# A fifth block of the first channel product computed from seven small products, and a second batch's x kept in DRAM

## The chip, the cores and the metric

The kernel runs on one core of one Trainium2 chip. The metric is device time in microseconds. One execution in the profile is a trace of every instruction on the core's engines: TensorE (PE for its matmuls, PEld for the loads of its stationary operand), VectorE (DVE), ScalarE (ACT), GpSimd (POOL) and SyncE (SP), which issues most transfers.

## The reference, cut to what matters

Inputs are q, k, v of shape (4, 8, 768, 64): batch, heads, sequence, head size. Each query and key is assigned to one of 16 clusters, attention is kept between equal clusters only, and the heads are put side by side to x of shape (4, 768, 512). A mixer block follows:

```
xt = x.transpose(0, 2, 1)
h = np.maximum(xt @ w_tok1, 0.0) @ w_tok2
u = x + h.transpose(0, 2, 1)
h2 = np.maximum(u @ w_ch1, 0.0) @ w_ch2
return (u + h2).astype(np.float32)
```

w_ch1 is 512 x 1536, w_ch2 is 1536 x 512, all in float32. The change lies in the product u @ w_ch1, here called the first channel product.

## The kernel before, in words

The program has three stages. Attention takes sixteen pairs of heads, up to about 316 us in the trace. The token stage (to about 394 us) computes the products with w_tok1 and w_tok2. The channel stage takes the rest.

The channel stage runs over the four batches in the order 0, 2, 3, 1, and in each over three parts. A part takes, by ch1_pair, one third of the columns of w_ch1, and then, by ch2_chunks, the second channel product for these columns, added to x. Products are made in blocks by a scheme with seven products in place of eight (Winograd's form of Strassen's): the table SEVEN names, for each of the seven, the PSUM tag, the left block or block sum (A11, S1 ...), the right one (B11, T1 ...) and where it goes. Left blocks come from the weights, and their sums are made once. Right blocks come from uT, the transposed u, and their sums are made for each batch by u_sums.

The first part of batch 0 runs ch1_plain: seven products, each for i = 0 and 1 (two halves of 128 of its columns), each with two matmuls of 128 x 384 that accumulate. The other eleven parts run ch1_sets, which goes one level deeper. It writes big(X, name, ...) for a product made plainly (A11 B11, S2 T2, S3 T3), and for the four others it takes "sets" of seven small products on blocks half as large (128 x 192 output): Y (A12 B21), P (S1 T1), Z (S4 B22) and X (A22 T4). set_lefts and set_rights build the block names, and left and right sums of a set (l2 in the tile w1ss, r2 in the tile uTss) are made by set_left_sums and set_right_sums on VectorE.

How a set is put together matters for the steps below. small(...) is one matmul. direct(bank, set) is two of them (c11 and c12) side by side in one bank. chain(q, set, name, x) makes one small product into the bank q, where the products of one set add up (p1, then u2, c22, c21), and then adds the bank, as it is at that moment, to x in SBUF with one VectorE sum. So the next product of the same chain can only start when that sum has read the bank. column(z, set, x) makes the product p5 and adds it to two places with one sum. relu and the copies run on ScalarE.

The order of work on each engine is the order in which the code records it; each engine takes its instructions in that order, and semaphores connect them. Between products, between() takes a recorded step from the list late (the rest of the part before) and some from others (sums for coming work), and big() also takes a step of beside, which turns the next batch's u.

Space in SBUF is given by pools that stand in a stack. The x of batches 1 and 3 share: xs lists four tiles, one of them (batch 1) in x1pool, which closes with the token stage; batch 1's x is written to the DRAM tile spill at the end of the first pair of batches, and read back into batch 0's tile after batch 0 is done. x of batch 3 stays in xpool. The pools w2sums (sums of w_ch2, w1ss, uTss) and mlp (the hidden blocks) take the space of the closed pools.

Lines to know in the profile: L798 is a big product, L871 a small one, L966 a product of ch2_chunks, L566 add and L563 sub on VectorE, L810 relu.

Of the kernel before, what the change touches and what calls it, by code (L numbers as in the profile page):

```python
# [8 lines left out]
F32 = mybir.dt.float32  # L9
# [10 lines left out]
P = 128  # L20
# [30 lines left out]
def kernel(  # L51
# [47 lines left out]
    x1pool = pool("x1pool", 1, tokens)  # L99
    spilled = pool("spilled", 1, space=bass.MemoryType.DRAM)  # L100
    tokpool = pool("tokpool", 1, tokens)
    staging = fast.enter_context(ExitStack())
    stage = pool("stage", 2, staging)
    attention = fast.enter_context(ExitStack())
# [25 lines left out]
    }  # L130

    state = {}
    spill = spilled.tile([P, NJ, DM], F32, name="spill")
    xs = [(x1pool if b == 1 else xpool).tile([P, NJ, DM], F32, name=f"x{b}") for b in range(B)]


    def load(g):
# [461 lines left out]

    def set_lefts():
        if "l2" not in pools:
            pools["l2"] = pools["w2sums"].tile([P, 4, 3, HS], F32, name="w1ss")
        l2 = pools["l2"]
        yx = W["ch1"].rearrange("p f (i r c) -> p f i r c", i=2, r=2)[:, 2:4]
        pz = pools["w1s"][:, 0:3:2].rearrange("p i f (r c) -> p f i r c", r=2)
        for n, both in enumerate((yx, pz)):
            blocks = [both[:, f, :, r] for r in range(2) for f in range(2)]
            sums_ = [l2[:, 2 * n : 2 * n + 2, m] for m in range(3)]  # L610
            yield dict(
                zip(("A11", "A12", "A21", "A22", "S1", "S2", "S4", "S3"), blocks + sums_ + blocks[2:3])
            )
# [6 lines left out]
    def set_rights():  # L620
        uT, R, r2 = pools["uT"], pools["R"], pools["r2"]
        yz = uT[:, :, 2:4].rearrange("p n f (k t) -> p n f k t", k=2)
        x, p = (R[name].rearrange("p f (k t) -> p f k t", k=2) for name in ("T4", "T1"))
        for blocks, sums_ in (
            ([yz[:, :, f, k] for f in range(2) for k in range(2)], [r2[:, 0:2, m] for m in range(3)]),
            ([x[:, f, k] for f in range(2) for k in range(2)], [r2[:, 2, m] for m in range(3)]),
            ([p[:, f, k] for f in range(2) for k in range(2)], [r2[:, 3, m] for m in range(3)]),
        ):
            yield dict(
                zip(("B11", "B12", "B21", "B22", "T1", "T2", "T4", "T3"), blocks + sums_ + blocks[1:2])  # L630
            )

    def set_right_sums():

        pools["r2"] = pools["w2sums"].tile([P, 4, 3, HS // 2], F32, name="uTss")
        return [list(winograd_right(blocks)) for blocks in set_rights()]

    def set_blocks():

        (yx, pz), (yz, x, p) = (list(y) for y in (set_lefts(), set_rights()))  # L640
        left = {name: {k: a[:, i] for k, a in two.items()} for two, i, name in
                ((yx, 0, "Y"), (yx, 1, "X"), (pz, 0, "P"), (pz, 1, "Z"))}
        right = {"Y": {k: b[:, 0] for k, b in yz.items()}, "Z": {k: b[:, 1] for k, b in yz.items()},
                 "X": x, "P": p}
        return left, right

    def token_weights():
# [98 lines left out]
    def by_turns(n, product, of, last=False, after=()):  # L746


        if last:
            order = "p1 0 p1 1 p1 2 p5 0 p5 1 p5 2 c11 0 c11 1 u2 0 u2 1 u2 2 c12 0 c12 1 c11 2 c12 2 "  # L750
            order += "c22 0 c22 1 c21 0 c22 2 c21 1 c21 2"
        else:
            order = "p1 0 p1 1 p1 2 p5 0 p5 1 p5 2 c11 0 c11 1 u2 0 u2 1 u2 2 c12 0 c12 1 "
            order += "c22 0 c22 1 c22 2 c12 2 c11 2 c21 0 c21 1 c21 2"
        order = order.split()
        banks, after = {}, dict(after)
        for m in range(len(order) // 2):
            name, i = order[2 * m], int(order[2 * m + 1])
            tag, a, r, to = SEVEN[name]
            if name in FIRST:  # L760
                banks[tag, i] = ptile(tag, n)
            product(banks[tag, i], a, r, i, name in FIRST)
            x = of(to, i)
            add(x, banks[tag, i], x)
            if m in after:
                after[m]()
            between()

    def tok2_chunks(b, after=()):

# [13 lines left out]
    def ch1_pair(part, sets, beside):  # L784


        h2 = pools["h2"] = {
            k: pools["mlp"].tile([P, 2, HS], F32, name="h" + k)
            for k in ("A11", "A12", "A22", "S1", "S2", "S3", "S4")
        }  # L790
        p5, c12 = (pools["mlp"].tile([P, 2, HS], F32, name=k) for k in ("p5", "c12"))
        A, R = pools["A"], pools["R"]
        a11, a12, a22 = h2["A11"], h2["A12"], h2["A22"]

        def product(psum, a, r, i, start):
            c = slice((part + 3 * i) * P, (part + 3 * i + 1) * P)
            for k in range(2):
                nc.tensor.matmul(  # L798
                    psum, lhsT=A[a][:, k, c], rhs=R[r][:, k],
                    start=start and k == 0, stop=k == 1, skip_group_check=not start,  # L800
                )

        def big(psum, a, r, i, start):
            product(psum, a, r, i, start)
            between()
            if a != "A11" and beside:
                beside.pop(0)()

        def relu(x):
            nc.scalar.activation(out=x, in_=x, func=ACT.Relu)  # L810


        def sum_1():
            nc.vector.scalar_tensor_tensor(
                out=h2["S1"], in0=c12, scalar=0.0, in1=a22, op0=ALU.max, op1=ALU.add
            )

        def sum_2():
            sub(h2["S2"], h2["S1"], a11)

        def sums_34():
            nc.vector.scalar_tensor_tensor(
                out=h2["S3"], in0=c12, scalar=0.0, in1=a11, op0=ALU.max, op1=ALU.subtract
            )
            sub(h2["S4"], a12, h2["S2"])

        (ch1_sets if sets else ch1_plain)(
            part, product, big, relu, a11, a12, a22, p5, c12, sum_1, sum_2, sums_34
        )

    def ch1_plain(part, product, big, relu, a11, a12, a22, p5, c12, sum_1, sum_2, sums_34):
        X, Z = {}, {}
        for i in range(2):
            X[i] = ptile("X", HS)
# [26 lines left out]
        late_(0)  # L861
        late.append(lambda: late_(1))

    def ch1_sets(part, product, big, relu, a11, a12, a22, p5, c12, sum_1, sum_2, sums_34):

        left, right = set_blocks()
        n0, n1 = slice(0, HS // 2), slice(HS // 2, HS)
# [45 lines left out]
        nc.scalar.copy(out=p5[:, 1, n1], in_=pz[:, n0])  # L913
        relu(a11[:, 0])
        add(p5[:, 0, n1], pz[:, n0], p5[:, 0, n1])
        add(c12[:, 0], X[0], p5[:, 0])
        big(X[1], "S2", "T2", 1, False)
        chain(yq, "Y", "c22", a11[:, 1, n1])
        chain(pq, "P", "c22", p5[:, 1, n1])
        direct(ybe, "Z")  # L920
        chain(yq, "Y", "c21", a11[:, 1, n0])
        small(pq[:, n0], "P", "c21", False)
        nc.scalar.copy(out=p5[:, 1, n0], in_=pq[:, n0])
        relu(a11[:, 1])
        add(c12[:, 0], ybe, c12[:, 0])
        chain(yz, "Z", "p1", c12[:, 0, n0])
        add(c12[:, 1], X[1], p5[:, 1])
        big(X[0], "S3", "T3", 0, False)
        add(a22[:, 0], X[0], p5[:, 0])
        relu(a22[:, 0])  # L930
        chain(yz, "Z", "u2", c12[:, 0, n1])
        column(pbe, "Z", c12)
        big(X[1], "S3", "T3", 1, False)
        add(a22[:, 1], X[1], p5[:, 1])
        relu(a22[:, 1])
        chain(yz, "Z", "c22", c12[:, 1, n1])
        direct(X[0], "X", False)
        nc.scalar.copy(out=a12[:, 0], in_=X[0])
        small(X[1][:, n0], "X", "c21", False)
        nc.scalar.copy(out=a12[:, 1], in_=X[1])  # L940
        chain(yz, "Z", "c21", c12[:, 1, n0])
        chain(yq, "X", "p1", a12[:, 0, n0])
        sum_1()

        def late_1():
            chain(yq, "X", "u2", a12[:, 0, n1])
            column(pz, "X", a12)
            sum_2()

        def late_2():  # L950
            chain(yq, "X", "c22", a12[:, 1].rearrange("p (k t) -> p k t", k=2))
            relu(a12)
            sums_34()

# [167 lines left out]
    for b in (0, 2):  # L1122
# [26 lines left out]
        if b == 2:  # L1149
            take(turning, len(turning))  # L1150
            usums = u_sums()
            tok2_chunks(b, {13: lambda: next(usums)})
        else:
            left_weights()
            others += left_sums(0)
            tok2_chunks(b)
            nc.sync.dma_start(spill, xs[1])
            turning = list(u_steps(0))
    assert not weights
    token_stack.close()  # L1160
# [5 lines left out]
    for n, b in enumerate(batches):  # L1166
        turning = []
        for part in range(3):
# [33 lines left out]
                (fits_count if part else fits)()  # L1202
            if part == 2 and not last:

                yz, x, p = steps
                yz[0]()
                yz[1]()
                next(usums)

                others += [lambda: next(usums)] * 2  # L1210
                others.append(lambda: [step() for step in (yz[2], p[2], yz[3], p[3])])
                others += [lambda: None, lambda: (x[0](), x[1]()), lambda: (x[2](), x[3]())]
                if n == 0:
                    xs[1] = xpool.tile([P, NJ, DM], F32, name="x0")
                    nc.sync.dma_start(xs[1], spill)


    def general():
# [213 lines left out]
```

## Time and profile before

The time is 823.15 us, the median of 3 runs (822.59 to 823.39). The profiled execution spans 821.6 us.

| engine | busy, us | share of the span | instructions |
|---|---|---|---|
| PE (matmuls) | 814.2 | 99% | 4348 |
| PEld (weight loads) | 535.5 | 65% | 4348 |
| DVE | 631.1 | 77% | 1206 |
| ACT | 374.7 | 46% | 573 |
| POOL | 30.7 | 4% | 28 |

The page's rows are groups of instructions: line, engine, operation, output and input by the program's names, count, busy time and mean duration in ns, and idle time before them with what ended it. A busy share is a mean over stages, so a stage is read from its own stretch of time. Matmuls overlap in the pipeline, so a row's mean duration (326 ns for 128 x 192, 486 for 128 x 384) is longer than the distance from one to the next. A float32 matmul of the program stands as two MATMULs in the trace. DMA moves 63.41 MB in all, most of it before the channel stage; the one spill of 1536 KB landed 5.1 us after its issue, and its load back 7.0 us after.

### The profile page before, as it was taken

Reading aid. Unit: us, or ns where it says so; the run is one execution under the profiler, and the core shown is the slowest. Engines: PE = TensorE matmul, PEld = TensorE weight load, DVE = VectorE, ACT = ScalarE, POOL = GpSimd, SP = SyncE. Lnnn points to the kernel's source line nnn. Section 1 sums busy time; section 2 is a strip of 40 time slices with the busy share of each in tenths; the row PEclk is TensorE's granted clock in tenths of the full one; section 3 lists DMA queues with packets and bytes.
Section 4 is the critical chain, followed back from the end, with each engine's and each line's share of the span. In section 5 each row is a group of like instructions: output and inputs, shape, how many; then the busy total and the mean of one; then the engine's idle time right before and its main releaser. Section 6 shows DMA issues by size and latency. Waiting matters only on the chain.

```text
span 821.6 us, 11693 instructions
## 1 busy us (share of the span) xinstructions
PE 814.2 (99%) x4348; PEld 535.5 (65%) x4348; DVE 631.1 (77%) x1206; ACT 374.7 (46%) x573; POOL 30.7 (4%) x28
## 2 busy tenths in 40 slices
PE   8999999999999999999999999999999999999997
PEld 4444444444444444444588888888888888888876
DVE  6879898989898978859797788755777566775665
ACT  5588776777878776127202154121441204511120
POOL 1001010111011000000000000000000000000000
PEclk9999999999999999999999999999999999999999
DMA  8797666768676434143000025000240001400002
GB/s 156 142 162 135 140 142 122 149 139 163 130 160 137 95 104 122 51 127 79 0 1 1 5 45 183 1 0 1 38 117 0 1 1 30 125 1 1 1 0 81
DMA packets 184258, 63.41 MB, mean 77 GB/s; under 512 B 172800, under 2 KB 176896, under 8 KB 183936
## 3 DMA queue, kind: packets, MB, share of 16 engines
q1 hardware_dynamic: 182592, 62.18, 34.7%
q8 instruction: 36, 0.59, 0.3%
q10 hardware_dynamic: 1600, 0.39, 0.2%
q14 instruction: 30, 0.25, 0.1%
HBM read 36.21 MB, written 7.86 MB: 54 GB/s over the span
## 4 chain that ended last, share of the span: by engine, by line
PE 98%; DVE 1%; issue 0%; ACT 0%; DVEq 0%; ACTq 0%
PE sc L413 19%; PE av L455 15%; PE pX L966 15%; PE pX L798 12%; PE pZ L966 7%; PE ph L534 5%; PE pY L871 5%; PE pZ L871 4%; PE pX L871 4%; PE pY L966 4%; PE pX L774 3%; PE small L491 2%; PE pZ L774 1%; PE small L304 1%; PE pZ L798 1%; PE pY L774 1%
## 5 line engine op out<-in xcount | busy, mean ns | idle before, releaser
L437 ACT ACTIVATE ex<-sc 128x768 f32<-128x768 f32 x192 | 151.0, 812 | 27.2 <-PE sc L413 15.5
L413 PE MATMUL sc<-qkT 64*128 64x384 f32 x768 | 155.3, 483 | 0.0
L445 DVE TENSOR_TENSOR sum<-sum,ex 128x768 f32<-128x768 f32 x128 | 127.8, 999 | 27.1 <-ACT ex L437 14.9
L455 PE MATMUL av<-ex,va 128*64 128x384 f32 x768 | 127.4, 488 | 0.0
L566 DVE TENSOR_TENSOR x<-pX,x 128x256 f32<-128x256 f32 (+1 forms) x168 | 75.8, 458 | 38.1 <-PE pX L966 37.6
L455 PEld LDWEIGHTS av<-ex,va 128*64 128x64 f32 x768 | 53.7, 137 | 71.7 <-issue 67.6
L413 PEld LDWEIGHTS sc<-qkT 64*128 64x128 f32 x768 | 67.8, 187 | 38.3 <-issue 38.0
L810 ACT ACTIVATE hA<-hA 128x384 f32<-128x384 f32 (+1 forms) x57 | 34.0, 597 | 85.4 <-DVE hA L566 85.1
L566 DVE TENSOR_TENSOR hA<-pY,hA 128x192 f32<-128x192 f32 (+1 forms) x90 | 36.7, 407 | 45.4 <-PE pY L871 42.7
L798 PE MATMUL pX<-uT,wc 128*128 128x384 f32 x192 | 69.8, 487 | 0.0
L894 ACT COPY hA<-pX 128x384 f32<-128x384 f32 x11 | 5.3, 479 | 131.3 <-PE pX L798 131.3
L413 PE MATMUL sc<-ohT 64*128 64x384 bf16 x384 | 62.4, 323 | 0.0
L462 ACT COPY avrows<-av 128x768 uint16<-128x768 uint16 x32 | 25.5, 797 | 44.4 <-PE av L455 44.4
L566 DVE TENSOR_TENSOR x<-pZ,x 128x256 f32<-128x256 f32 (+1 forms) x84 | 36.4, 455 | 11.4 <-PE pZ L966 11.3
L798 PEld LDWEIGHTS pX<-uT,wc 128*128 128x128 f32 x192 | 35.4, 190 | 14.7 <-issue 0.6
L534 PE MATMUL ph<-x,wt 128*128 128x512 f32 x96 | 41.6, 593 | 0.0
L413 PEld LDWEIGHTS <-ohT 64*128 64x128 bf16 x384 | 18.7, 94 | 33.8 <-issue 9.6
L966 PE MATMUL pX<-wc,hA 128*128 128x256 f32 x144 | 36.9, 380 | 0.3 <-ACT hA L940 0.3
L711 ACT COPY uT<-ucols 128x768 uint16<-128x768 uint16 x32 | 33.2, 1049 | 4.7 <-DMA ucols<-urows 4.7
L966 PE MATMUL pZ<-wc,hS 128*128 128x256 f32 x144 | 35.0, 379 | 0.0
L966 PE MATMUL pY<-wc,hA 128*128 128x256 f32 x144 | 35.0, 379 | 0.0
L798 PE MATMUL pX<-uTs,w1s 128*128 128x384 f32 x96 | 34.9, 486 | 0.0
(189 smaller groups left out, 1310.8 us busy)
## 6 DMA issues: line engine op xcount, KB each, us to landing
raw<-in_moe_w_ch_dram SPq DMA_DIRECT2D x24, 512.0 KB, 4.5
va<-in_v_dram SPq DMA_DIRECT2D x16, 384.0 KB, 3.7
out_dram<-x SPq DMA_DIRECT2D x24, 256.0 KB, 2.3
qk<-in_k_dram SPq DMA_DIRECT2D x60, 96.0 KB, 4.0
qk<-in_q_dram SPq DMA_DIRECT2D x60, 96.0 KB, 3.5
raw<-in_moe_w_tok_dram SPq DMA_DIRECT2D x3, 512.0 KB, 4.1
raw<-in_moe_w_tok_dram SPq DMA_DIRECT2D x4, 384.0 KB, 3.8
spill<-x SPq DMA_DIRECT2D x1, 1536.0 KB, 5.1
```

What stands on the lines that cost most here:

```text
L413: nc.tensor.matmul(sc[:, h, 0:HS], lhsT=src[rows, 1, j], rhs=src[rows, 0, HJ * qh : HJ * qh + HJ], start=start, stop=not start,)
L437: nc.scalar.activation(out=ex, in_=sc[:, :, 0:HS], func=ACT.Exp, scale=SM_SCALE)
L445: nc.vector.tensor_tensor(out=acc, in0=acc if j > 1 else st["ex", qh, 0], in1=st["ex", qh, j], op=ALU.add)
L455: nc.tensor.matmul(av[h * D : (h + 1) * D], lhsT=st["va"][:, h, j], rhs=ex[:, h], start=(j == 0), stop=(j == NJ - 1),)
L534: nc.tensor.matmul(pf, lhsT=W["tok1"][:, j, t * P : (t + 1) * P], rhs=xs[b][:, j], start=(j == 0), stop=(j == NJ - 1),)
L566: nc.vector.tensor_tensor(out=dst, in0=a, in1=b, op=ALU.add)
L711: nc.scalar.copy(out=out, in_=pools.pop(("ucols", i)).rearrange("p w j t -> p w (j t)"))
L774: nc.tensor.matmul(psum, lhsT=A[a][:, i], rhs=R[r], start=start, stop=True, skip_group_check=not start,)
L798: nc.tensor.matmul(psum, lhsT=A[a][:, k, c], rhs=R[r][:, k], start=start and k == 0, stop=k == 1, skip_group_check=not start,)
L810: nc.scalar.activation(out=x, in_=x, func=ACT.Relu)
L871: nc.tensor.matmul(psum, lhsT=left[which][a][:, part * P : part * P + P], rhs=right[which][r], start=start, stop=True, skip_group_check=no ...
L966: nc.tensor.matmul(psum, lhsT=h2[a][:, k, i * P : (i + 1) * P], rhs=Bw[w][:, part + 3 * k], start=start and k == 0, stop=k == 1, skip_grou ...
```

## The change

A fifth of the seven products of the first channel product, S3 T3, is no longer made by big products but as a set, U, of seven small ones. Its bank is not shared with the other big products as before: U is put together in a new SBUF tile u3, like P in p5, and added from there to a22 and a12. S3 is a block of w_ch1 itself, T3 a block of u's sums; U's own sums need a fifth place in w1ss and in uTss. The set's products are recorded among those of Y and Z, so the second half of ch1_sets has a new order. To make room in SBUF, x of batch 3 also goes into a pool that closes after the token stage; it is written to DRAM at the end of the token stage and read back after batch 0, and batch 1 is then read back after batch 2. The remaining edits spread recorded steps: by_turns now passes between() a number that empties others over its steps, and a new helper aside() takes a step of beside.

```diff
-    spill = spilled.tile([P, NJ, DM], F32, name="spill")
-    xs = [(x1pool if b == 1 else xpool).tile([P, NJ, DM], F32, name=f"x{b}") for b in range(B)]
+    spill = {b: spilled.tile([P, NJ, DM], F32, name=f"spill{b}") for b in (1, 3)}
+    homes = (xpool, x1pool, xpool, x3pool)
+    xs = [homes[b].tile([P, NJ, DM], F32, name=f"x{b}") for b in range(B)]
...
-            pools["l2"] = pools["w2sums"].tile([P, 4, 3, HS], F32, name="w1ss")
+            pools["l2"] = pools["w2sums"].tile([P, 5, 3, HS], F32, name="w1ss")
...
+            ([u[:, f, k] for f in range(2) for k in range(2)], [r2[:, 4, m] for m in range(3)]),
...
-            between()
+            between(-(-len(others) // max(len(order) // 2 - m, 1)))
...
-        add(c12[:, 0], X[0], p5[:, 0])
+
+        add(a22[:, 0], X[0], p5[:, 0])
         big(X[1], "S2", "T2", 1, False)
         chain(yq, "Y", "c22", a11[:, 1, n1])
         chain(pq, "P", "c22", p5[:, 1, n1])
-        direct(ybe, "Z")
+        direct(ybe, "U")
+        nc.scalar.copy(out=u3[:, 0], in_=ybe)
         chain(yq, "Y", "c21", a11[:, 1, n0])
         small(pq[:, n0], "P", "c21", False)
         nc.scalar.copy(out=p5[:, 1, n0], in_=pq[:, n0])
         relu(a11[:, 1])
-        add(c12[:, 0], ybe, c12[:, 0])
-        chain(yz, "Z", "p1", c12[:, 0, n0])
-        add(c12[:, 1], X[1], p5[:, 1])
-        big(X[0], "S3", "T3", 0, False)
-        add(a22[:, 0], X[0], p5[:, 0])
+        chain(pbe, "U", "p1", u3[:, 0, n0])
+        add(a22[:, 1], X[1], p5[:, 1])
+        nc.scalar.copy(out=c12[:, 1], in_=a22[:, 1])
+        between()
+        direct(pz, "Z")
+        chain(pbe, "U", "u2", u3[:, 0, n1])
+        add(c12[:, 0], pz, a22[:, 0])
+        small(yz[:, n0], "U", "p5")
+        nc.scalar.copy(out=u3[:, 1, n1], in_=yz[:, n0])
+        add(u3[:, 0, n1], yz[:, n0], u3[:, 0, n1])
+        chain(yq, "Z", "p1", c12[:, 0, n0])
+        chain(pbe, "U", "c22", u3[:, 1, n1])
+        add(a22[:, 0], a22[:, 0], u3[:, 0])
+        chain(yq, "Z", "u2", c12[:, 0, n1])
+        between()
+        small(pbe[:, n0], "U", "c21", False)
+        nc.scalar.copy(out=u3[:, 1, n0], in_=pbe[:, n0])
         relu(a22[:, 0])
-        chain(yz, "Z", "u2", c12[:, 0, n1])
-        column(pbe, "Z", c12)
-        big(X[1], "S3", "T3", 1, False)
-        add(a22[:, 1], X[1], p5[:, 1])
+        column(pq, "Z", c12)
+        chain(yq, "Z", "c22", c12[:, 1, n1])
+        add(a22[:, 1], a22[:, 1], u3[:, 1])
         relu(a22[:, 1])
-        chain(yz, "Z", "c22", c12[:, 1, n1])
         direct(X[0], "X", False)
-        nc.scalar.copy(out=a12[:, 0], in_=X[0])
+        add(a12[:, 0], X[0], u3[:, 0])
         small(X[1][:, n0], "X", "c21", False)
-        nc.scalar.copy(out=a12[:, 1], in_=X[1])
-        chain(yz, "Z", "c21", c12[:, 1, n0])
-        chain(yq, "X", "p1", a12[:, 0, n0])
+        add(a12[:, 1], X[1], u3[:, 1])
+        chain(yq, "Z", "c21", c12[:, 1, n0])
+        chain(ybe, "X", "p1", a12[:, 0, n0])
         sum_1()
+        aside()
...
+            nc.sync.dma_start(spill[3], xs[3])
         else:
...
-            nc.sync.dma_start(spill, xs[1])
+            nc.sync.dma_start(spill[1], xs[1])
...
-                others += [lambda: None, lambda: (x[0](), x[1]()), lambda: (x[2](), x[3]())]
-                if n == 0:
-                    xs[1] = xpool.tile([P, NJ, DM], F32, name="x0")
-                    nc.sync.dma_start(xs[1], spill)
+                others += [lambda: (u[0](), u[1]()), lambda: (u[2](), u[3]())]
+                others.append(lambda: [step() for step in x])
+                if n < 2:
+
+                    later = batches[n + 2]
+                    xs[later] = xpool.tile([P, NJ, DM], F32, name=f"x{b}")
+                    nc.sync.dma_start(xs[later], spill[later])
```

More of the change, by code (lines that the diff above doesn't have):

```diff
@@ L101 @@
     tokpool = pool("tokpool", 1, tokens)
+    x3pool = pool("x3pool", 1, tokens)
     staging = fast.enter_context(ExitStack())
@@ L603, in set_lefts @@
         if "l2" not in pools:
-            pools["l2"] = pools["w2sums"].tile([P, 4, 3, HS], F32, name="w1ss")
+            pools["l2"] = pools["w2sums"].tile([P, 5, 3, HS], F32, name="w1ss")
         l2 = pools["l2"]
-        yx = W["ch1"].rearrange("p f (i r c) -> p f i r c", i=2, r=2)[:, 2:4]
+        w1 = W["ch1"].rearrange("p f (i r c) -> p f i r c", i=2, r=2)
         pz = pools["w1s"][:, 0:3:2].rearrange("p i f (r c) -> p f i r c", r=2)
-        for n, both in enumerate((yx, pz)):
+        for n, both in ((slice(0, 2), w1[:, 2:4]), (slice(2, 4), pz), (slice(4, 5), w1[:, 0:2, 1:2])):
             blocks = [both[:, f, :, r] for r in range(2) for f in range(2)]
-            sums_ = [l2[:, 2 * n : 2 * n + 2, m] for m in range(3)]
+            sums_ = [l2[:, n, m] for m in range(3)]
             yield dict(
@@ L622, in set_rights @@
         yz = uT[:, :, 2:4].rearrange("p n f (k t) -> p n f k t", k=2)
-        x, p = (R[name].rearrange("p f (k t) -> p f k t", k=2) for name in ("T4", "T1"))
+        x, p, u = (R[name].rearrange("p f (k t) -> p f k t", k=2) for name in ("T4", "T1", "T3"))
         for blocks, sums_ in (
@@ L633, in set_right_sums @@
     def set_right_sums():
-        pools["r2"] = pools["w2sums"].tile([P, 4, 3, HS // 2], F32, name="uTss")
+        pools["r2"] = pools["w2sums"].tile([P, 5, 3, HS // 2], F32, name="uTss")
         return [list(winograd_right(blocks)) for blocks in set_rights()]
     def set_blocks():
-        (yx, pz), (yz, x, p) = (list(y) for y in (set_lefts(), set_rights()))
-        left = {name: {k: a[:, i] for k, a in two.items()} for two, i, name in
-                ((yx, 0, "Y"), (yx, 1, "X"), (pz, 0, "P"), (pz, 1, "Z"))}
+        (yx, pz, u), (yz, x, p, ur) = (list(y) for y in (set_lefts(), set_rights()))
+        left = {name: {k: a[:, i] for k, a in some.items()} for some, i, name in
+                ((yx, 0, "Y"), (yx, 1, "X"), (pz, 0, "P"), (pz, 1, "Z"), (u, 0, "U"))}
         right = {"Y": {k: b[:, 0] for k, b in yz.items()}, "Z": {k: b[:, 1] for k, b in yz.items()},
-                 "X": x, "P": p}
+                 "X": x, "P": p, "U": ur}
         return left, right
@@ L790, in ch1_pair @@
         }
-        p5, c12 = (pools["mlp"].tile([P, 2, HS], F32, name=k) for k in ("p5", "c12"))
+        p5, u3, c12 = (pools["mlp"].tile([P, 2, HS], F32, name=k) for k in ("p5", "u3", "c12"))
         A, R = pools["A"], pools["R"]
@@ L801, in product, with aside @@
                 )
+        def aside():
+            if beside:
+                beside.pop(0)()
         def big(psum, a, r, i, start):
@@ L805, in big @@
             between()
-            if a != "A11" and beside:
-                beside.pop(0)()
+            if a != "A11":
+                aside()
         def relu(x):
@@ L825, in sums_34, with ch1_plain @@
             sub(h2["S4"], a12, h2["S2"])
+        more = (u3, aside) if sets else (product,)
         (ch1_sets if sets else ch1_plain)(
-            part, product, big, relu, a11, a12, a22, p5, c12, sum_1, sum_2, sums_34
+            part, big, relu, a11, a12, a22, p5, c12, sum_1, sum_2, sums_34, *more
         )
-    def ch1_plain(part, product, big, relu, a11, a12, a22, p5, c12, sum_1, sum_2, sums_34):
+        assert not beside
+    def ch1_plain(part, big, relu, a11, a12, a22, p5, c12, sum_1, sum_2, sums_34, product):
         X, Z = {}, {}
@@ L862, in ch1_plain, with ch1_sets @@
         late.append(lambda: late_(1))
-    def ch1_sets(part, product, big, relu, a11, a12, a22, p5, c12, sum_1, sum_2, sums_34):
+    def ch1_sets(part, big, relu, a11, a12, a22, p5, c12, sum_1, sum_2, sums_34, u3, aside):
         left, right = set_blocks()
@@ L924, in ch1_sets @@
         relu(a11[:, 1])
-        add(c12[:, 0], ybe, c12[:, 0])
-        chain(yz, "Z", "p1", c12[:, 0, n0])
-        add(c12[:, 1], X[1], p5[:, 1])
-        big(X[0], "S3", "T3", 0, False)
-        add(a22[:, 0], X[0], p5[:, 0])
+        chain(pbe, "U", "p1", u3[:, 0, n0])
[15 more added lines that the diff above has]
+        nc.scalar.copy(out=u3[:, 1, n0], in_=pbe[:, n0])
         relu(a22[:, 0])
-        chain(yz, "Z", "u2", c12[:, 0, n1])
-        column(pbe, "Z", c12)
-        big(X[1], "S3", "T3", 1, False)
-        add(a22[:, 1], X[1], p5[:, 1])
+        column(pq, "Z", c12)
+        chain(yq, "Z", "c22", c12[:, 1, n1])
+        add(a22[:, 1], a22[:, 1], u3[:, 1])
         relu(a22[:, 1])
-        chain(yz, "Z", "c22", c12[:, 1, n1])
         direct(X[0], "X", False)
-        nc.scalar.copy(out=a12[:, 0], in_=X[0])
+        add(a12[:, 0], X[0], u3[:, 0])
         small(X[1][:, n0], "X", "c21", False)
-        nc.scalar.copy(out=a12[:, 1], in_=X[1])
-        chain(yz, "Z", "c21", c12[:, 1, n0])
-        chain(yq, "X", "p1", a12[:, 0, n0])
+        add(a12[:, 1], X[1], u3[:, 1])
+        chain(yq, "Z", "c21", c12[:, 1, n0])
+        chain(ybe, "X", "p1", a12[:, 0, n0])
         sum_1()
+        aside()
         def late_1():
-            chain(yq, "X", "u2", a12[:, 0, n1])
+            chain(ybe, "X", "u2", a12[:, 0, n1])
             column(pz, "X", a12)
@@ L950, in late_2 @@
         def late_2():
-            chain(yq, "X", "c22", a12[:, 1].rearrange("p (k t) -> p k t", k=2))
+            chain(ybe, "X", "c22", a12[:, 1].rearrange("p (k t) -> p k t", k=2))
             relu(a12)
@@ L1203 @@
             if part == 2 and not last:
-                yz, x, p = steps
+                yz, x, p, u = steps
                 yz[0]()
```

## The prediction

> **What bounds the kernel now.** I read the engine totals first, then who TensorE waited for, then stretches of one part of the channel stage, then its instructions in order of time.
>
> ```profile
> PE 814.2 (99%) x4348; PEld 535.5 (65%) x4348; DVE 631.1 (77%) x1206; ACT 374.7 (46%) x573; POOL 30.7 (4%) x28
> ```
>
> The waits of TensorE (who waited for whom: us in total, times, longest):
>
> ```profile
> PE av L1032 <- DVE warm L1019: 1.2, 1, 1.2
> PE pr L304 <- DVE qkT L1042: 0.5, 1, 0.5
> PE pt L376 <- ACT qkT L1038: 0.4, 1, 0.4
> PE pX L966 <- ACT hA L940: 0.3, 1, 0.3
> ```
>
> TensorE is the bound: busy 99%, and four waits of 2.4 us in all, three of them in the start. So a matmul less is worth its length, and a matmul that has to wait costs its wait. Now one part of the channel stage (520.31 to 555.28), and in it the first and second half of the first channel product:
>
> ```profile
> 520.31:555.28 34.97, 34.97 (x166) 29.61 (x165) 21.73 (x50) 5.55 (x12) 0.00 (x0) 1.00 0.00 1
> 537.00:544.10 7.10, 7.10 (x34) 5.51 (x32) 3.10 (x8) 2.18 (x5) 0.00 (x0) 1.00 0.00 0
> 544.10:551.55 7.45, 7.45 (x39) 6.39 (x38) 4.92 (x13) 2.42 (x6) 0.00 (x0) 1.00 0.00 1
> ```
>
> Columns: length, then busy time (and instructions) of PE, PEld, DVE, ACT, POOL. Over the part VectorE has 13 us to spare, but in the second half, the stretch that the change rewrites, it is at 4.92 of 7.45: 2.5 us spare. The steps of that stretch:
>
> ```profile
> 544.10 0.49 PE L871 MATMUL pY<-uT,wc 128*128 128x192 f32 x2
> ...
> 544.42 0.49 PE L871 MATMUL pZ<-uTs,w1s 128*128 128x192 f32 x2
> ...
> 545.40 0.49 PE L871 MATMUL pY<-uTss,wc 128*128 128x192 f32 x2
> ...
> 545.92 0.36 DVE L566 TENSOR_TENSOR hA<-pY,hA 128x192 f32<-128x192 f32 x1 [0.62 <-PE pY L871]
> ...
> 546.20 0.55 DVE L566 TENSOR_TENSOR c<-pY,c 128x384 f32<-128x384 f32 x1
> ...
> 547.86 0.56 DVE L566 TENSOR_TENSOR hA<-pX,p 128x384 f32<-128x384 f32 x1 [0.19 <-PE pX L798]
> ...
> 548.34 0.35 DVE L566 TENSOR_TENSOR c<-pX,c 128x192 f32<-128x192 f32 x1
> ```
>
> One f32 product shows as two MATMULs. A small product (192 columns) starts 0.325 after the one before (the 0.32 and 0.33 of these starts); a big one (384) takes 0.645. A small one's result is complete 0.49 after its start (545.40 to 545.89), and the sum that reads it starts 0.03 to 0.04 later (545.92). Back to back, VectorE starts the next sum 0.28 after a 192-column one and 0.48 after a 384-column one, some 0.085 before the shown end. What a late sum costs TensorE:
>
> ```profile
> 514.90 0.55 DVE L566 TENSOR_TENSOR hA<-pX,p 128x384 f32<-128x384 f32 x1
> ...
> 515.50 0.30 PEld L871 LDWEIGHTS pX<-uTss,wc 128*128 128x128 f32 x2 [0.34 <-DVE hA L566]
> 515.50 0.59 PE L871 MATMUL pX<-uTss,wc 128*128 128x192 f32 x2
> ...
> 515.93 0.49 PE L871 MATMUL pX<-uTss,w1s 128*128 128x192 f32 x2
> ```
>
> The sum ends at 515.45, the weight load that waited starts 0.054 later, and the pair takes 0.43 instead of 0.325: its load, else beside the matmul before it, is exposed. So a waiting product is as good as started 0.054 + 0.104 = 0.158 after the sum.
>
> [...]
>
> **The change part by part.** "Set" parts are the 11 of 12 that run ch1_sets.
>
> Removed, TensorE: the two big S3T3 products, 2 x 2 x 0.645 = 2.58 a part. Added: seven small ones of set U, 7 x 0.325 = 2.275. Gain 0.305 a part, 11 x 0.305 = 3.36 us.
>
> VectorE, in the stretch: before, five sums of 384 columns use X and S3T3 (two into c12, one from Y, two into a22). After, seven of 384 (a22 twice, c12 once, a22 += u3 twice, a12 twice) and four more of 192 for U. That is 2 x 0.472 + 4 x 0.272 = 2.03 us, against 2.5 spare. From Y's c21 sum to X's p1 sum there are ten of 192 and seven of 384: 10 x 0.272 + 7 x 0.472 = 6.02, beside 18 small products, 18 x 0.325 = 5.85. So VectorE becomes as long as TensorE there even without a gap, and gaps there are, since sums and products wait for each other along the chains (a product adds into the bank that a sum has just read). ScalarE gets 2 copies of 192 columns more (0.32 each), with half its time free.
>
> The walk of a part without other sums in it (a second or third one), t = 0 at Y's c22 product. On TensorE the order is Yc22, Pc22, U direct (2), Yc21, Pc21, U p1 (1.95), Z direct (2.275, 2.60), U u2, U p5, Z p1, U c22, Z u2, U c21, Z p5, Z c22, X direct (2), X c21, Z c21, X p1, two products of 0.432 of the second channel product, X u2.
> - U p1 is complete at 2.44; its sum runs 2.48 to 2.83; U u2 can start at 2.83 + 0.158 = 2.99, is due at 2.925: wait 0.07.
> - U p5 3.32, Z p1 3.64 (complete 4.13). VectorE meanwhile: U u2's sum 3.52 (its product is complete at 3.48), c12 = Z + a22 at 3.79, U p5's sum at 4.26, and only then Z p1's, 4.53 to 4.89.
> - U c22 waits for U u2's sum (3.87): 0.07, done 4.36.
> - Z u2 is next and due at 4.36; it needs Z p1's sum: 4.89 + 0.158 = 5.05. Wait 0.69. Behind it stand U c21, Z p5, Z c22 and all that follows: nobody fills in.
> - Z c22 waits for Z u2's sum, 5.57 to 5.93: 0.07.
> - X u2 is due at 8.90; VectorE, without a pause since 5.57, ends X p1's sum at 9.13: wait 0.38.
>
> Sum 0.07 + 0.07 + 0.69 + 0.07 + 0.38 = 1.27 (with unrounded terms). Less 0.305: a part gets 0.97 longer. Eight such parts: 7.7 us.
>
> The first parts of the three later batches also carry the right-hand set sums. Before, such a part (590.25 to 625.67) took 35.42, 0.45 over an undisturbed 34.97. After, the block U adds four sums of 192 columns, and all x and u sums fall into the stretch (the change moves them to the new gaps): eight sums at 0.27, 2.1 us of VectorE that a plain part does not have, in line with the chains' own sums. The same walk gives waits of 0.24, 0.07, 0.30, 0.69, 0.07, 0.20, 0.54 and 0.44 = 2.54; less the 0.45 it had and the 0.305: 1.79 a part, three parts 5.4.
>
> In the first batch, 12 left-hand sums for U of 128 columns [...] go into the steps between products. Where they fall beside the second channel product VectorE has room; once they push a sum of x back far enough that a product waits, 0.3 by the same walk [...].
>
> The spill: batch 3's x leaves at about 392.1, after its last sum; a spill took 5.1 us to land, so 397.2. Of the tiles laid over it w1ss is written first, at 401.35 today: hidden by the w2s sums. If it took the 7.0 us of the load back, still hidden. The loads back start when a batch's output has left, at about 503 and 608, and are first read a batch later, some 80 us on. Cost 0 (upper bound 2). New gap calls in by_turns take one step each while no more steps wait than slots: 0.
>
> Sum: 7.7 + 5.4 + 0.3 = +13.4 us, 836.6.
>
> **The rivals.**
> (1) The waits come out shorter: the 0.104 of load hides, and VectorE's starts are a little earlier. With 0.054 in place of 0.158 the walk gives a part 0.65 + 0.03 + 0.31 = 1.0 and a first part 2.3; net 8 x 0.69 + 3 x 1.55 = 10.2: 833.3. With half of all waits it is 823.15 + 0.5 x (8 x 1.27 + 3 x 2.54) - 3.36 - 3 x 0.45 = 827.3. For it: the margins are tenths. Against: the exposed load above. 0.17 for under 831.
> (2) Not slower: the sums hide and 3.36 is gained, 819.8. For it: VectorE is at 62% of a part. Against: the stretch's 6.02 beside 5.85 and the chain Z p1 to Z u2 with one product between. 0.06.
> (3) Longer: the first parts' sums pile up further, or the spill holds VectorE (up to 2 us), or disturbed loads expose more: 841 to 845. 0.09.
>
> **How the numbers follow.** The forecast 0.68 at 836.6, the rivals 0.17, 0.06 and 0.09. The range from 829.5 to 840.5 takes in the forecast and most of rival 1 and leaves out some 2 in 10. Faster by over 0.2% needs nearly all of the gain: 0.05; within 0.2%: 0.02; slower 0.93.
>
> **What would show it.** Parts of 35.9 and 37 us in place of 34.97 and 35.4; waits of TensorE on VectorE in the small-product line, some 0.7 before Z's u2 in every set part, 0.4 before X's u2; 44 big matmuls gone and 77 small ones come, counted by program; VectorE busy in the stretch without a pause. I am wrong if the small products keep their 0.325 through the stretch, or if VectorE runs the sums closer than 0.27 and 0.47.

## The result, and the profile after

The kernel after the change takes 838.17 us (837.74 to 838.40, six runs), the one before 823.00 us beside it (822.59 to 823.47, six runs): ratio 1.0183, 95% interval 1.0170 to 1.0196. It is slower by 15.1 us; the prediction said 13.4 (836.6), with a range of 829.5 to 840.5.

The engine totals of the kernel after, and from the same page the shares of the chain that ended last (who did the work, or was waited for, on the way back from the last instruction):

```profile
PE 821.7 (98%) x4414; PEld 541.1 (65%) x4414; DVE 658.1 (79%) x1300; ACT 383.4 (46%) x595; POOL 30.7 (4%) x28
...
PE 91%; DVE 7%; issue 1%; ACT 0%; DVEq 0%
```

The same shares in the kernel before:

```profile
PE 98%; DVE 1%; issue 0%; ACT 0%; DVEq 0%; ACTq 0%
```

There are 66 MATMULs more, as 77 small products for 44 big ones make at two MATMULs each. They should make TensorE's work shorter; its busy time grew by 7.5 us, because part of each wait counts as busy: a product whose weight load waited is shown for longer (0.59 in place of 0.49), and a product is shown for 0.49 although the next could start after 0.325. With hardly any such waits the same products are busy 812.0, in the last but one experiment. The shares say it better: VectorE's part of the chain that ended last grew from 1% to 7%.

Who TensorE waited for, in the kernel after (us in total, times, longest):

```profile
PE pY L881 <- DVE c L568: 5.4, 14, 0.4
PE av L1055 <- DVE warm L1042: 1.2, 1, 1.2
PE pY L881 <- DVE hA L568: 0.6, 3, 0.2
PE pr L306 <- DVE qkT L1065: 0.5, 1, 0.5
```

The first and third line are new: small products (line 881) that wait for a VectorE sum (line 568) into the tile c12 (shown as c, its number left out) or into a hidden block (hA). The view counts only time in which TensorE had nothing at all in flight, so its 6 us are less than half of the loss. I therefore took the whole loss from the distances between the starts of successive products, against 0.325 for a small and 0.432 or 0.645 for the others.

One part of the channel stage of the kernel after, and in it the rewritten stretch (length, then busy time and instructions of PE, PEld, DVE, ACT, POOL):

```profile
560.68:596.71 36.03, 35.48 (x171) 30.12 (x171) 23.58 (x56) 8.51 (x17) 0.00 (x0) 1.00 0.09 17
584.46:592.57 8.11, 7.71 (x46) 7.01 (x45) 6.26 (x17) 3.48 (x9) 0.00 (x0) 1.00 0.14 27
```

A part went from 34.97 to 36.03. In the stretch VectorE is busy 6.26 of 8.11, where before it was 4.92 of 7.45. Lengths of the eleven set parts, from the first product of one second channel product to the first of the next:

| part | before | after | difference |
|---|---|---|---|
| the two set parts of the first batch | 70.66 | 72.77 | 2.11 |
| first parts of the later batches | 35.27, 35.42, 35.28 | 37.53, 37.52, 37.53 | 2.26, 2.10, 2.25 |
| the five other parts but the last | 34.97 each | 36.03 each | 1.06 each |
| the last part | 35.54 | 36.49 | 0.95 |

The differences add up to 2.11 + 6.61 + 5.30 + 0.95 = 15.0, so the whole loss lies in the eleven set parts.

The largest wait of a plain part, before Z's u2 (start, duration, engine, line, operation; in brackets the idle time before it and what ended it), in the kernel after:

```profile
588.18 0.49 PE L881 MATMUL pY<-uT,w1s 128*128 128x192 f32 x2
588.33 0.55 DVE L568 TENSOR_TENSOR c<-pZ,hA 128x384 f32<-128x384 f32 x1
...
588.50 0.56 PE L881 MATMUL pZ<-uT,wc 128*128 128x192 f32 x2
588.79 0.35 DVE L568 TENSOR_TENSOR u<-pX,u 128x192 f32<-128x192 f32 x1
589.06 0.35 DVE L568 TENSOR_TENSOR c<-pY,c 128x192 f32<-128x192 f32 x1
...
589.46 0.59 PE L881 MATMUL pY<-uTss,w1ss 128*128 128x192 f32 x2 [0.40 <-DVE c L568]
```

Read it by the tile pY. Z's p1 starts at 588.18 and is complete at 588.67. The sum that reads it could start at 588.70; but VectorE has the sum into c12 (588.33) and that of U's p5 (588.79) in front of it, both recorded ahead of it, and starts it at 589.06. It ends at 589.41, and Z's u2, which adds into the same bank, starts at 589.46 with its weight load exposed. In between TensorE did a single product, U's c22 at 588.50. From due time to effective start this is 0.67.

### The profile page after: what moved, and what is told of

The parts are those of the page before. It is cut to its first block, busy times and chain, and to the rows that moved or that the text cites. A ratio compares the mean times of both kernels' runs of the same rounds, so it can differ in the third digit from the quotient of the medians.

```text
span 836.3 us, 11988 instructions
## 1 busy us (share of the span) xinstructions
PE 821.7 (98%) x4414; PEld 541.1 (65%) x4414; DVE 658.1 (79%) x1300; ACT 383.4 (46%) x595; POOL 30.7 (4%) x28
## 4 chain that ended last, share of the span: by engine, by line
PE 91%; DVE 7%; issue 1%; ACT 0%; DVEq 0%
PE sc L415 19%; PE av L457 15%; PE pX L989 13%; PE pX L802 7%; PE pZ L989 7%; PE pZ L881 6%; PE pY L881 5%; PE ph L536 5%; PE pY L989 4%; DVE hA L568 3%; PE pX L778 2%; DVE c L568 2%; PE small L493 1%; PE pZ L778 1%; PE small L306 1%
## 5 line engine op out<-in xcount | busy, mean ns | idle before, releaser
L802 PE MATMUL pX<-uT,wc 128*128 128x384 f32 x104 | 37.8, 487 | 0.0
L989 PE MATMUL pX<-wc,hS 128*128 128x256 f32 x144 | 33.3, 380 | 0.1
```

What stands on the lines that cost most here:

```text
L802: nc.tensor.matmul(psum, lhsT=A[a][:, k, c], rhs=R[r][:, k], start=start and k == 0, stop=k == 1, skip_group_check=not start,)
L989: nc.tensor.matmul(psum, lhsT=h2[a][:, k, i * P : (i + 1) * P], rhs=Bw[w][:, part + 3 * k], start=start and k == 0, stop=k == 1, skip_grou ...
```

## The experiments

The kernel before, run again on the same chip, took 823.06 us (822.55 to 823.79) beside the spill, U's sums, the moved products and the new order, and 823.28 (822.55 to 824.21) beside the other four. "Part" below is the distance used in the table above.

### The spill alone

The kernel before with batch 3's x in a pool of its own, its store after the token stage and its load after batch 0.

```
+    x3pool = pool("x3pool", 1, tokens)
...
+    homes = (xpool, x1pool, xpool, x3pool)
...
+            nc.sync.dma_start(spill[3], xs[3])
...
+                if n < 2:
+                    later = batches[n + 2]
+                    xs[later] = xpool.tile([P, NJ, DM], F32, name=f"x{b}")
+                    nc.sync.dma_start(xs[later], spill[later])
```

> The kernel before with only the memory move: x of batch 3 in a pool that closes after the token stage, spilled and read back. Theory (the lost time is TensorE waiting for late VectorE sums in the rewritten stretch): no change, 823.0 within 0.5. Rival (the spill holds the first sums of the channel stage, or the loads back disturb): 825 or more.

Measured: 823.13 us (822.21 to 823.33), ratio 0.9999 (0.9990 to 1.0007), parts unchanged at 34.97. In the trace of the kernel after, the store of batch 3's x is issued at 392.1 and lands 5.0 us later, at 397.2, while w1ss, which by the prediction is the first tile written over its space, is first written at 401.3, as in the kernel before (401.35). The spill costs nothing.

### U's own sums alone

The kernel before with the spill, and with U's left and right sums made in steps near those of the change, but not needed by any product. The rest of the stretch keeps its old order, and the right-hand sums of U and X are shared out over the steps a little differently than in the change. S3 and T3 of U's own sums are written onto a block of w_ch1 and a block of u's sums, in place; the big product S3 T3, which stays here, and later products on those blocks then multiply overwritten data. The number of products and their order are those of the kernel before.

```
-            pools["l2"] = pools["w2sums"].tile([P, 4, 3, HS], F32, name="w1ss")
+            pools["l2"] = pools["w2sums"].tile([P, 5, 3, HS], F32, name="w1ss")
...
+            ([u[:, f, k] for f in range(2) for k in range(2)], [r2[:, 4, m] for m in range(3)]),
...
-                others += [lambda: None, lambda: (x[0](), x[1]()), lambda: (x[2](), x[3]())]
+                others += [lambda: (u[0](), u[1]()), lambda: (u[2](), u[3](), x[0](), x[1]()), lambda: (x[2](), x[3]())]
```

> The kernel before with the memory move and with set U's own left and right sums made in the slots of the change, but not used; S3 T3 stays a big product. Theory: these sums fall into slots where VectorE has room for most of them, some waits in the parts of the first batch: 823 to 825.5. Rival (the sums that U needs are the cost, not its putting together): 830 or more.

Measured: 826.32 us (825.99 to 826.99), ratio 1.0039 (1.0026 to 1.0053): 0.8 above the top of what was expected. Plain parts stay at 34.97; the first parts become 36.25, 36.26 and 36.25 (0.83 to 0.98 more), the first batch 71.01 (0.35 more). TensorE's waits in this kernel:

```profile
PE pX L874 <- DVE hA L568: 1.3, 3, 0.4
...
PE pY L874 <- DVE hA L568: 0.5, 3, 0.2
```

Three times each: once in each first part. So U's own sums cost 3.3 us when they are put into the old order, nearly all in the first parts, and nothing of what a plain part lost. In the kernel after, a first part lost 1.0 to 1.2 more than a plain one, somewhat above the 0.83 to 0.98 here; how much of it is theirs in the new order, no run separates.

### X's first two products between Z's p1 and u2

The kernel after, with two products moved to where Z's u2 waits. If the wait belonged to that one chain, two products of 0.325 would fill it.

```
         chain(yq, "Z", "p1", c12[:, 0, n0])
+        direct(X[0], "X", False)
         chain(pbe, "U", "c22", u3[:, 1, n1])
...
-        direct(X[0], "X", False)
         add(a12[:, 0], X[0], u3[:, 0])
```

> The changed kernel with one reorder: the two direct products of set X stand between Z's p1 and Z's u2, where TensorE waited 0.67 us in every set part. If only the latency of that one chain costs, the wait is filled: 11 x 0.65 less, 831. If VectorE is short of time in the whole stretch, the wait turns up again further on (X's sum into a12 then comes earlier in the queue than the sums of Z): 838 to 841.

Measured: 840.58 us (840.40 to 841.13), ratio 1.0215 (1.0201 to 1.0229). A plain part takes 36.33, not 36.03. The wait before Z's u2 fell from 0.67 to 0.08, but its waits together rose from 1.35 to 1.66. The products of the swapped kernel:

```profile
589.58 0.49 PE L881 MATMUL pZ<-uT,wc 128*128 128x192 f32 x2
589.90 0.57 PE L881 MATMUL pY<-uTss,w1ss 128*128 128x192 f32 x2
590.51 0.59 PE L881 MATMUL pZ<-uTss,wc 128*128 128x192 f32 x2
...
591.27 0.57 PE L881 MATMUL pY<-uT,w1s 128*128 128x192 f32 x2
591.67 0.49 PE L881 MATMUL pX<-uTss,wc 128*128 128x192 f32 x2
592.54 0.59 PE L881 MATMUL pY<-uTss,w1s 128*128 128x192 f32 x2 [0.38 <-DVE c L568]
```

Again by tiles. U's c22 and c21 (pZ at 589.58 and 590.51) have one product between them, as in the kernel after; there the wait before that product, Z's u2, had covered the link, and now U's c21 pays 0.31. Z's c22 and c21 (pY at 591.27 and 592.54) had three products between them and now have one: they pay 0.65. So one wait had hidden a second one, and the moved products had served as filling elsewhere: the wait went to these two places.

What such a link costs can be put together from rows already shown: 0.49 until the product is complete, 0.035 to the start of its sum, 0.355 for the sum, 0.158 to the effective start of the next product, 1.04 in all, if VectorE is free at once. Three small products between hide it (1.30 from start to start), two leave 0.065 (0.975), one leaves 0.39 (0.65). Of the 0.65 just seen, the other 0.26 is VectorE's queue: the sum of Z's c22 starts at 592.13, behind the one of Z's p5 into c12. The waits of 0.066 and 0.068 before U's c22 and Z's c22 in the kernel after are just such links with two between. So Z's u2 with its 0.67 lost 0.32 by having one product between (0.39 less the 0.066 that U's c22, the one between, had already waited), and 0.355 because VectorE took its sum at 589.06 and not at 588.70.

### Two sums fewer, and the same two on GpSimd

The kernel after without the two sums of u3 into a22, which are then missing from that block; and the kernel after with these two sums on GpSimd.

```
-        add(a22[:, 0], a22[:, 0], u3[:, 0])
...
-        add(a22[:, 1], a22[:, 1], u3[:, 1])
```

> The changed kernel without the two sums a22 += u3 (so the hidden block A22 lacks U's share): two VectorE instructions of 384 columns, 0.93 us, less in a set part; TensorE's work and the chains stay. If VectorE is short of time in the stretch: the wait before X's u2 (0.41) nearly goes, in first parts more, by the walk 3.6 us less: 834.5. If only the latency from product to sum to product counts, these two sums stand on no chain and nothing changes: 838.

Measured: 834.59 us (834.25 to 835.16), ratio 1.0138 (1.0123 to 1.0154). A plain part takes 35.68, a first part 37.11. The wait of 0.41 before X's u2 has shrunk to 0.06; that before Z's u2, whose sum is recorded ahead of these two, stays at 0.67. In the kernel after, the wait before X's u2 looks like this:

```profile
593.34 0.35 DVE L568 TENSOR_TENSOR hA<-pY,hA 128x192 f32<-128x192 f32 x1
593.74 0.19 PEld L881 LDWEIGHTS pY<-uTss,w1ss 128*128 128x128 f32 x1 [0.55 <-DVE hA L568]
```

X's p1 and X's u2 have two of the second channel product's products between them (0.432 each), 1.19 from start to start, so the link of 1.04 alone would cost nothing: this wait was VectorE's queue alone.

```
+        nc.gpsimd.tensor_tensor(out=a22[:, 0], in0=a22[:, 0], in1=u3[:, 0], op=ALU.add)
...
+        nc.gpsimd.tensor_tensor(out=a22[:, 1], in0=a22[:, 1], in1=u3[:, 1], op=ALU.add)
```

> The changed kernel with the two sums a22 += u3 on GpSimd, idle in this stage; the trace of before has 1.17 us for a GpSimd sum of 384 columns. Theory: VectorE is relieved as in the run that leaves them out, and relu of a22 comes in time for S1: 834.5. Rival: GpSimd slows VectorE by as much, or its sum comes late for S1: 837 to 841.

Measured: 837.40 us (836.65 to 837.51), ratio 1.0168 (1.0155 to 1.0182). The number is the rival's in the expectation. A plain part takes 35.71, nearly as without the sums (35.68). But a first part takes 37.94, 0.41 more than in the kernel after and 0.83 more than without the sums. In the kernel with GpSimd, a stretch of a first part:

```profile
626.49 0.36 DVE L565 TENSOR_TENSOR uTss<-uTs,uTss 128x192 f32<-128x192 f32 x1
626.55 1.15 POOL L957 TENSOR_TENSOR hA<-hA,u 128x384 f32<-128x384 f32 x1 [0.59 <-ACT u L953]
626.76 1.15 DVE L565 TENSOR_TENSOR uTs<-uTs 128x192 f32<-128x192 f32 x1
...
627.84 0.35 DVE L565 TENSOR_TENSOR uTss<-uTs,uTss 128x192 f32<-128x192 f32 x1
```

The VectorE sum of 626.76, with both inputs in SBUF, takes 1.15 in place of 0.35 and ends 0.2 after GpSimd's; TensorE then waits 1.0 before X's c21, where it waited 0.2 in the kernel after. The same happens once in each of the three first parts. In the other parts no such sum stands beside GpSimd's, only sums that read a bank in PSUM, and these keep their 0.35 to 0.36 (0.56 for 384 columns). So of the 3.6 us that leaving out the two sums gains, three first parts give back 2.5.

### X's rest one step later

The kernel after with the last steps of a set part (X's u2 and what follows it) recorded one step further into the second channel product, except in the first batch.

```
-        late.extend([late_1, late_2])
+        late.extend([lambda: None] * (pools["n"] > 0) + [late_1, late_2])
...
+            pools["n"] = n
```

> The changed kernel with the rest of set X taken one step later in the second channel product (not in the first batch). VectorE then has 0.86 us more before X's u2: the wait there (0.41 in the plain parts, 0.41 in the first ones) goes, nothing else moves. Nine parts x 0.36, by the walk 3.1 less: 835. If TensorE's time is lost elsewhere than in these waits: 838.

Measured: 836.07 us (835.81 to 836.41), ratio 1.0154 (1.0140 to 1.0168). This is 1.1 above what was expected, since something else did move. A plain part takes 35.74, 0.30 less: X's u2 no longer waits (0.41 less), and 0.94 of the waits is left, but a product of the second channel product now waits 0.10 for relu. The first parts take 37.12 to 37.23.

### All products in another order

The same products, sums and copies as in the kernel after, recorded in an order in which a product that needs a sum has at least two others between it and the one before it in its chain, mostly more (a big product counts as two); the places where a step of other work is taken move with them; with X's rest later as above, and three sums for the next batch inside the second channel product and not behind it. It was chosen with the durations of the prediction's walk. Cut to the stretch with U and Z:

```
+        small(pbe[:, n0], "U", "p1")
+        small(pq[:, n0], "P", "u2", False)
+        small(yq[:, n0], "Y", "c22", False)
+        big(X[0], "S2", "T2", 0, False)
+        small(yq[:, n0], "Y", "c21", False)
+        small(pq[:, n0], "P", "c22", False)
+        add(u3[:, 0, n0], pbe[:, n0], u3[:, 0, n0])
+        small(pbe[:, n0], "U", "u2", False)
+        small(pz[:, n0], "Z", "c11")
+        small(pz[:, n1], "Z", "c12")
+        small(yq[:, n0], "Z", "p1")
+        add(u3[:, 0, n1], pbe[:, n0], u3[:, 0, n1])
+        small(yz[:, n0], "U", "p5")
+        small(pq[:, n0], "P", "c21", False)
+        big(X[1], "S2", "T2", 1, False)
+        add(c12[:, 0], pz, a22[:, 0])
+        add(c12[:, 0, n0], yq[:, n0], c12[:, 0, n0])
+        add(a22[:, 0], a22[:, 0], u3[:, 0])
+        small(pbe[:, n0], "U", "c22", False)
+        small(yq[:, n0], "Z", "u2", False)
+        small(pq[:, n0], "Z", "p5")
+        small(X[0][:, n0], "X", "c11", False)
+        small(X[0][:, n1], "X", "c12", False)
+        small(pbe[:, n0], "U", "c21", False)
+        small(yq[:, n0], "Z", "c22", False)
+        small(ybe[:, n0], "X", "p1")
+        small(X[1][:, n0], "X", "c21", False)
+        small(yq[:, n0], "Z", "c21", False)
...
+                after[16] = lambda: next(usums)
+                after[18] = lambda: steps[0][0]()
+                after[19] = lambda: steps[0][1]()
```

(Sums, copies and relu that stand between these lines are left out.)

> The changed kernel with the same products, sums and copies in another order: U, P and Y are begun early, in the first half of the first channel product, where VectorE has 4 us to spare, X's direct and the others fill the gaps of the Z chain; the rest of X is taken one step later in the second channel product (not in the first batch), and three sums of the next batch one step earlier. Theory (the cost is where the sums stand, not how many they are): the waits vanish but for some 0.1 to 0.6 a part, and the 3.36 us of shorter products come through in part: 820.5 to 823, best guess 821.5. Rival (VectorE has too much to do with U in whatever order, or small products cost TensorE more than 0.325): 830 or more.

Measured: 821.33 us (820.88 to 822.13, twelve runs), ratio to the kernel before 0.9979 (0.9971 to 0.9988): faster than both. TensorE's waits in the reordered kernel:

```profile
PE av L1078 <- DVE warm L1065: 1.2, 1, 1.2
PE pX L1012 <- ACT hA L818: 0.8, 1, 0.8
PE pr L306 <- DVE qkT L1088: 0.5, 1, 0.5
PE pt L378 <- ACT qkT L1084: 0.4, 1, 0.4
```

No small product is on this list any more. The distances between starts still show 0.23 before U's u2 in each first part, and 0.27 before X's u2 in the two set parts of the first batch, where X's rest is not moved. In the same kernel, one plain part, and two overlapping stretches inside another:

```profile
624.47:659.21 34.74, 34.74 (x172) 30.27 (x171) 23.12 (x56) 6.23 (x14) 0.00 (x0) 1.00 0.00 1
577.00:586.00 9.00, 9.00 (x49) 7.79 (x48) 7.09 (x19) 4.28 (x10) 0.00 (x0) 1.00 0.36 46
581.00:589.00 8.00, 8.00 (x42) 7.04 (x42) 7.75 (x19) 3.87 (x9) 0.00 (x0) 1.00 0.17 28
```

TensorE is busy 34.74 of 34.74. The part has 56 VectorE instructions, like that of the kernel after, and in the first stretch VectorE is busy 79% of the time (7.09 of 9.00), against 77% (6.26 of 8.11) in the rewritten stretch of the kernel after. In the second it is busy 97% (7.75 of 8.00), and TensorE still 8.00 of 8.00. So as much work on VectorE does no harm by itself; where each product and sum stands does. A part is 34.74 = 34.97 - 0.305 + 0.067, where 0.067 is the one wait left, before Z's c21, again a link with two products between. In the last part 0.8 is lost before the second channel product, waiting for relu; the kernel before has 0.3 there.

### The other edits of that kernel, put into the kernel before

X's rest one step later and the three sums earlier, with S3 T3 as two big products.

```
-        late.extend([late_1, late_2])
+        late.extend([lambda: None] * (pools["n"] > 0) + [late_1, late_2])
...
+                after[16] = lambda: next(usums)
+                after[18] = lambda: steps[0][0]()
+                after[19] = lambda: steps[0][1]()
```

> The kernel before (S3 T3 big) with the two side edits of the reordered kernel: the rest of X one step later, three sums of the next batch one step earlier. It tells what of the reordered kernel's gain over before belongs to U. Before has 1 us of such waits in all: 822.5 to 823.1. If it reaches 821.3, U brings nothing even in the new order.

Measured: 823.09 us (822.50 to 823.62), ratio 0.9999 (0.9991 to 1.0007). On the kernel before, these edits are worth nothing, so what the reordered kernel gained on it belongs to the set U in its new order. The new order with S3 T3 as two big products was not run; but in a plain part of the kernel before no product starts more than 0.03 later than the length of the one before it allows, so no other order of these products could have gained the 0.23 there.

## Why the prediction was right, by its own steps

- The gain of 3.36 us (0.305 a part): right, but in the kernel after it is hidden behind the waits. In the reordered kernel plain parts are shorter than before by 0.23, which is 0.305 less the one wait left.
- Plain set parts, waits of 1.27 and a net 0.97: measured 1.35 and 1.06. One by one (forecast, measured): U u2 0.07, 0.14; U c22 0.07, 0.07; Z u2 0.69, 0.67; Z c22 0.07, 0.07; X u2 0.38, 0.41. The term most mis-sized is that of U's u2. U's p1 is complete at 586.90, and its sum starts 0.11 later, not 0.035; the profile names a ScalarE copy as what came last:

```profile
587.01 0.36 DVE L568 TENSOR_TENSOR u<-pZ,u 128x192 f32<-128x192 f32 x1 [0.36 <-ACT p L935]
```

The prediction had no wait of VectorE on ScalarE in its walk.
- First parts, waits of 2.54 and a net 1.79: measured 2.85 and 2.10 to 2.26. The largest miss is Y's c21, 0.24 forecast and 0.45 measured: Y's sum could have started at 621.02, when its product (from 620.50) was complete, but stands behind a sum into a22 and two of the batch's own right-hand sums, of which this is the second:

```profile
621.46 0.36 DVE L565 TENSOR_TENSOR uTss<-uT,uTss 128x192 f32<-128x192 f32 x1
621.74 0.35 DVE L568 TENSOR_TENSOR hA<-pY,hA 128x192 f32<-128x192 f32 x1
```
```profile
622.14 0.59 PE L881 MATMUL pY<-uTss,wc 128*128 128x192 f32 x2 [0.18 <-DVE hA L568]
```

Besides, the prediction subtracted 0.45 for waits that the part of 590.25 to 625.67 had before. The other two first parts (35.27 and 35.28) had only 0.31, which makes their net longer by 0.14 each.

- The first batch's left-hand sums, 0.3: its two parts lost 2.11, twice what a plain part loses, so 0 is left for the sums (twelve of 128 columns, 0.28 to 0.29 each in the kernel after). Alone in the kernel before, U's sums did cost that batch 0.35.
- The spill, 0: measured 0.
- The sum: the prediction counted 8 x 0.97 + 3 x 1.79 + 0.3 = 13.4. Measured it is 2.11 + 5 x 1.06 + 0.95 + 6.61 = 15.0. Of the 1.6 between, 1.2 is the first parts (0.9 longer waits, 0.3 the waits wrongly subtracted) and 0.6 the eight others, less the 0.3 of the first batch. Apart from those 0.3, all these errors go the same way; that the 0.3 went the other way and brought the sum nearer was luck.

One reason the prediction gave did not hold as it stood: that VectorE becomes as long as TensorE in the stretch. Its 6.02 beside 5.85 were counted rightly for the recorded order, but VectorE was not busy without a pause there: from Y's c21 sum (586.29) to X's p1 sum (593.34) it stood still for 1.0 us in four pauses, waiting in its turn. And the reordered kernel runs as dense a VectorE with a full TensorE. What held is the other half of that argument, the chains with one product between, together with sums standing behind others in VectorE's queue. How the loss divides between the two is shown by the trace for two waits: 0.32 and 0.355 before Z's u2, the queue alone before X's u2.

Of the rivals, shorter waits (827 to 833) fails on the load of 0.104, which was exposed in full at every wait of a small product over 0.1 us in the parts read; "not slower" on the waits themselves. "Longer" (841 to 845) was half right in its place, the first parts, and too large. That a plain part's loss comes from the spill or from U's own sums is excluded by their runs, and a dearer small product by the reordered kernel, where the same products fill a part without a gap.

## What to carry to other kernels

When matmul work is cut up into smaller products that meet in one bank, count for each link how many other products lie between (here the link took 1.04 us, some three small products), and then which sums stand ahead of its own in the queue; a part's mean load, 62% of VectorE before, does not tell. Filling one gap with work taken from another moves the wait; an order that keeps two or more products in every link, and takes X's rest later (worth 2.1 us alone on the kernel after), turned the same work from 15.1 us slower to 1.7 us faster. Test side edits alone, so that a gain is put down to the right one.

## What the runs showed of the hardware

In the kernel with the two sums on GpSimd, a VectorE sum of 128 x 192 with both inputs in SBUF took 1.15 us in place of 0.35; it began 0.21 us after a GpSimd sum of 128 x 384 (626.76, 626.55) and ended 0.21 after it (627.91, 627.70). This happened once in each of the three first parts: the eight VectorE sums of this form (uTs<-uTs) average 0.651 there, as three of 1.15 and five of 0.35 do, and 0.352 in the kernel after. A sum with two SBUF inputs that had begun 0.06 before GpSimd's (626.49) kept its 0.36. In a plain part, VectorE's sums with one input in PSUM kept their time beside GpSimd's sum (590.16 to 591.16): 0.56 for the 384 columns begun at 590.09, 0.36 for the 192 begun at 590.75. No run varied the place of the inputs alone, so what made the three sums longer is not shown beyond this.

GpSimd's sums of 128 x 384 took 1.00 us (the 1.17 of the expectation was of an int32 operation) where no such VectorE sum began beside them and 1.15 in these three cases, against 0.55 on VectorE. In the plain parts the slower sums cost next to nothing: 35.71 with them, 35.68 without them.
